# The last 96 rows of a down projection: chunks 0 and 1 in pieces of 32 rows, and the last token tile's feed-forward sum taken out of its bank whole

## The chip, the cores and the metric

The kernel runs on one core of one Trainium2 chip. The metric is the device time of one execution in microseconds (us). A kernel is executed several times and the median counts; one further execution is recorded by the hardware profiler, and all views below come from that one.

TensorE (PE) multiplies matrices into PSUM, which this kernel uses as eight banks of 128 x 512 fp32 values. ScalarE (ACT) and VectorE (DVE) read PSUM and work on SBUF. GpSimd (POOL) does a few small operations here and issues DMAs from its own queue, as SyncE (SP) and ACT do from theirs. Each engine and each queue works in order.

## The reference

For one sequence of 2048 tokens with 512 features the kernel adds a residual, a state-space layer and a gated feed-forward layer, the two layers both reading the layer-normed input:

```python
x = A_x                                   # 1 x 2048 x 512
xn = _layernorm(x, axis=-1)
# A: h[t] = Lam_bar * h[t-1] + B_bar xn[t] (complex, 512 states); y = 2 Re(C h) + xn * Dskip
# B: (silu(xn @ w_gate) * (xn @ w_up)) @ w_down        with F = 1376 hidden columns
return x + A(xn) + B(xn)
```

F = 1376 is 10 full tiles of 128 hidden columns and a remainder of 96. The change is about these 96 rows of `w_down`.

## The kernel before

**Tiles.** The 2048 tokens are 4 chunks (`NCH`) of 512 tokens (`CW`), each of 4 token tiles (`TPC`) of 128. Normed tokens lie transposed in `xnT`. Everything is written out by hand: an outer list of calls sets PE's order, and DVE's state-space work stands in a `backlog` that `pump` works off beside PE's matmuls and `need(tag)` forces to its end. The tile layer keeps this order and puts in the waits; the pool `psum` has 8 buffers, one per bank.

**Stages of a chunk.** `bproj_chunk(c)` projects the input to the states (32 matmuls, L371). `gateup_chunk(c)` makes gate and up of the feed-forward layer: first `gateup_last(c)` (L501, the remainder of 96 columns, packed into one bank with a part of up), then 10 tiles of 2 x 4 matmuls (L446). ACT takes each bank out (silu L460, copy L461), DVE multiplies pairs of them (L465). The product of the remainder stands in `gu_last` (96 rows x 512 tokens; `product_last`, L477). Then the down projection sums, for each token tile, 10 matmuls of 128 x 512 (L587 in `out_ffn` for chunks 0 and 1, L559 in `out_pair` for chunks 2 and 3) and the 96 remaining rows, and the 8 matmuls of the state-space output (L606, `out_ssm`) are added in the same bank.

**The remainder, two ways.** `out_last` (L594) multiplies it with one more matmul per token tile: `gu_last`, whose rows 96 to 127 are set to zero by DVE at the start (L170), against slice `FT - 1` of `wd_sb`. Chunk 1 does this in `out_ffn`. Chunk 0 does it late, in `out_end(0)`, after the first tile of chunk 2's gate and up, because the up part of its remainder is made only in `up_halves` (L490); until then its four sums stay in their banks. Chunks 2 and 3 do it in pieces (`out_rows`, L547): `move_rows` copies the product by 12 DMAs on POOL (L186) so that each of the four token tiles has its own group of 32 partitions, `load_rows` (L180, POOL) puts the 96 rows of `w_down` four times into the dead space of `BT`, and each of three steps then runs four matmuls of 32 rows, one for each token tile, in the four row groups of PE.

**The last token tile.** Tile 15 is summed in two column halves (`col_parts`): columns 256 to 511 first, closed by one `out_last` of 256 columns, then columns 0 to 255, for which the pieces are used. `part_end` (DVE, L575) takes the upper half out of the bank with the skip part added; the state-space matmuls of the last 256 columns run in two fresh banks of 128 columns (`out_blocks`), those of the first half go on in the old bank. L611 adds and casts, L614 stores.

**Leaving.** Chunks 0 to 2 leave through `out_leave`: an ACT copy (L619) into `res` (pool `opool`, 6 buffers) and a DMA on POOL that adds to `out` in DRAM (L620). `skip_store` (L530, POOL) adds the skip part the same way.

**PE's order around the change:** ... B-projection 2, `out_chunk(0)` = 40 x L587, `up_halves`, 32 x L606; gate and up of chunk 2 with `out_end(0)` in it; B-projection 3; `load_rows`; `out_chunk(1)` = 4 x (10 x L587 + 1 x L594), 32 x L606; gate and up of chunk 3; `out_pair(2)`.

Of the kernel before, what the change touches and what calls it, by code (L numbers as in the profile page):

```python
# [10 lines left out]
F32 = mybir.dt.float32  # L11
BF16 = mybir.dt.bfloat16
ALU = mybir.AluOpType
ACT = mybir.ActivationFunctionType
# [9 lines left out]
def kernel(  # L24
# [17 lines left out]
    nc = tc.nc  # L42
# [30 lines left out]
    def bank(shape=(128, CW), dtype=F32):  # L73
        return psum.tile(list(shape), dtype, name="ps")
# [18 lines left out]
        wu_g.append(const.tile([128, KD, cols], BF16, name=f"wu{gi}"))  # L93
    w_last = const.tile([128, KD, 128], BF16, name="w_last")
    wu_last = const.tile([128, KD, LB], BF16, name="wu_last")
    wd_sb = const.tile([128, FT, D], BF16, name="wd_sb")
    BT = const.tile([128, 2, KD, Pst], BF16, name="BT")
    CT = const.tile([128, 2, NQ, D], BF16, name="CT")
    dsk_bc = const.tile([128, D], BF16, name="dsk_bc")
# [48 lines left out]
    def load_late():  # L148
        nc.sync.dma_start(out=wu_last[:], in_=wu_v[:, :, FL:FL + LB])
        nc.sync.dma_start(out=xall[:, 2 * TPC:NT, :], in_=x_v[:, 2 * TPC:NT, :])  # L150
        nc.sync.dma_start(out=wd_sb[:, 0:nfull, :], in_=B_w_down[0:nfull * 128, :].rearrange("(k p) d -> p k d", p=128))
        if nfull < FT:
            nc.sync.dma_start(out=wd_sb[0:F - FL, nfull, :], in_=B_w_down[FL:F, :])

    nfull = F // 128


    ones = nc.const_aps.tensor(1.0, (128, CW), BF16)
# [6 lines left out]

    gu_last = [const.tile([128, CW], BF16, name=f"gu_last{i}") for i in range(3)]
    for t in (*(g[LB + LA:128, :] for g in gu_last), wd_sb[LB + LA:128, FT - 1, :]):
        nc.vector.memset(t, 0.0)  # L170


    RT = 32
    part_end = const.tile([128, D // 2], F32, name="part_end")
    gu_rows = [const.tile([128, 3, 128], BF16, name=f"gu_rows{i}") for i in range(2)]
    wd_rows = BT[:, 0, 0:3, :]

    def load_rows():
        for i in range(TPC):
            nc.gpsimd.dma_start(out=wd_rows[i * RT:(i + 1) * RT], in_=B_w_down[FL:F, :].rearrange("(p f) d -> f p d", f=RT))  # L180

    def move_rows(c):

        for i in range(TPC):
            for p in range(3):
                nc.gpsimd.dma_start(out=gu_rows[c % 2][i * RT:(i + 1) * RT, p, :],  # L186
                                    in_=gu_last[c % 3][p * RT:(p + 1) * RT, i * 128:(i + 1) * 128])

    stats = const.tile([128, NT, 6], F32, name="stats")
    stats_1 = const.tile([128, 2, 6], F32, name="stats_1")  # L190
# [278 lines left out]
    def ul(c):  # L469
        if c not in up_last:  # L470
            up_last[c] = up_p.tile([128, CW], BF16, name="ul", bufs=4)
        return up_last[c]

    def product_last(c):
        g, u = gu_last[c % 3][0:LB + LA, :], ul(c)[0:LB + LA, :]
        def mul():
            V.tensor_tensor(out=g, in0=g, in1=u, op=ALU.mult)  # L477
            if c > 1:
                move_rows(c)
        products.append(mul)  # L480

    def up_halves():
# [15 lines left out]
    def gateup_last(c):  # L498
        ps = bank()
        for k in range(KD):  # L500
            nc.tensor.matmul(ps[:], lhsT=w_last[:, k, :], rhs=xnT[:, k, c * CW:(c + 1) * CW],  # L501
                             start=(k == 0), stop=(k == KD - 1))
        u = ul(c)
        nc.scalar.activation(out=gu_last[c % 3][0:LB + LA, :], in_=ps[0:LB + LA], func=ACT.Silu)
        nc.scalar.copy(out=u[LB:LB + LA, :], in_=ps[LB + LA:128])
        if c > 1:
            product_last(c)
# [27 lines left out]
    def out_blocks(n):  # L535

        return ((0, D // 2), (D // 2, D - 128), (D - 128, D)) if n == NT - 1 else ((0, D),)

    def col_parts(n):
        return ((D // 2, D), (0, D // 2)) if n == NT - 1 else ((0, D),)  # L540

    def out_rows(c, step):

        for i in range(TPC):
            n, rows = c * TPC + i, slice(i * RT, (i + 1) * RT)
            lo, hi = col_parts(n)[-1]
            nc.tensor.matmul(o_tiles[n][0][:, lo:hi], lhsT=gu_rows[c % 2][rows, step, :],  # L547
                             rhs=wd_rows[rows, step, lo:hi], start=False, stop=False)

    def out_pair(c):  # L550

        multiply(0)
        for n in range(c * TPC, (c + 2) * TPC):
            o = bank()
            o_tiles[n] = [o]
            k, i = divmod(n, TPC)
            for lo, hi in col_parts(n):
                for fi in range(FT - 1):
                    nc.tensor.matmul(o[:, lo:hi], lhsT=gu_tiles[k][:, fi, i * 128:(i + 1) * 128],  # L559
                                     rhs=wd_sb[:, fi, lo:hi], start=(fi == 0), stop=False)  # L560
                if lo > 0:
                    out_last(n, o[:, lo:hi], lo, hi, True)
            pump(FT * 0.2163)
        for step in range(3):
            for k in (c, c + 1):
                out_rows(k, step)
        need(f"ssm{c}")
        need("skip")
        for n in range(c * TPC, (c + 1) * TPC):
            out_ssm(n)  # L570
            pump(2 * NQ * 0.2163)
        need(f"ssm{c + 1}")
        n = NT - 1
        o = o_tiles[n][0]
        V.tensor_tensor(out=part_end[:], in0=o[:, D // 2:D], in1=xn_end[:, TPC - 1, D // 2:D], op=ALU.add)  # L575
        o_tiles[n] = [o, *(bank((128, hi - lo)) for lo, hi in out_blocks(n)[1:])]
        for n in range((c + 1) * TPC, (c + 2) * TPC):
            out_ssm(n)

    def out_ffn(n):  # L580
        c, i = divmod(n, TPC)
        o_tiles[n] = []
        for lo, hi in out_blocks(n):
            o = bank((128, hi - lo))
            o_tiles[n].append(o)
            for fi in range(FT - 1):
                nc.tensor.matmul(o[:], lhsT=gu_tiles[c][:, fi, i * 128:(i + 1) * 128], rhs=wd_sb[:, fi, lo:hi],  # L587
                                 start=(fi == 0), stop=False)
            if c > 0:
                out_last(n, o, lo, hi, False)  # L590

    def out_last(n, o, lo, hi, stop):
        c, i = divmod(n, TPC)
        nc.tensor.matmul(o[:], lhsT=gu_last[c % 3][:, i * 128:(i + 1) * 128], rhs=wd_sb[:, FT - 1, lo:hi],  # L594
                         start=False, stop=stop)

    def out_ssm(n):
        c, i = divmod(n, TPC)
        if c > 0:
            res = opool.tile([128, D], BF16, name="res")  # L600
        for o, (lo, hi) in zip(o_tiles[n], out_blocks(n)):
            fresh = n == NT - 1 and lo > 0
            o = o[:, 0:hi - lo]
            for part in range(2):
                for q in range(NQ):
                    nc.tensor.matmul(o, lhsT=w_tiles[c][:, part, q, i * 128:(i + 1) * 128],  # L606
                                     rhs=CF[:, part, q, lo:hi], start=(fresh and part == 0 and q == 0),
                                     stop=(c > 0 and part == 1 and q == NQ - 1))
            if c == NCH - 1:
                rest = part_end[:, lo - D // 2:hi - D // 2] if fresh else xn_end[:, i, lo:hi]  # L610
                V.tensor_tensor(out=res[:, lo:hi], in0=o, in1=rest, op=ALU.add)  # L611
                for a, b in ((0, D // 2), (D // 2, D)) if i == 0 else ((lo, hi),):
                    late = b == D and n in (NT - TPC, NT - 1)
                    (nc.sync if late else nc.scalar).dma_start(out=out_v[:, n, a:b], in_=res[:, a:b])  # L614
            elif c > 0:
                out_leave(n, o, res)

    def out_leave(n, o, res):
        nc.scalar.copy(out=res[:], in_=o[:])  # L619
        nc.gpsimd.dma_start(out=out_v[:, n, :], in_=res[:], accum_op=ALU.add)  # L620
# [31 lines left out]
    def multiply(keep):  # L652

        while len(products) > keep:
            products.pop(0)()
            owed[0] -= 0.65

    def need(tag):

        while any(item[3] == tag for item in backlog):  # L660
            step()
# [98 lines left out]
    def gateup_chunk(c):  # L760
        for fi in [FT - 1, *range(FT - 1)]:
            gateup_tile(c, fi)
            pump(GU)
            multiply(1)
            if c == 2 and fi == 0:
                out_end(0)

    def out_chunk(c):

        multiply(0)  # L770
        for n in range(c * TPC, (c + 1) * TPC):
            out_ffn(n)
            pump(FT * 0.2163)
        if c == 0:
            need("ln3")
            up_halves()
            multiply(0)
        need(f"ssm{c}")
        need("cf")
        for n in range(c * TPC, (c + 1) * TPC):  # L780
            out_ssm(n)
            pump(2 * NQ * 0.2163)

    def out_end(c):

        for n in range(c * TPC, (c + 1) * TPC):
            o = o_tiles[n][0]
            out_last(n, o, 0, D, True)
            out_leave(n, o, opool.tile([128, D], BF16, name="res"))

    def spread(ops, others, tag, tags):

# [90 lines left out]
```

## Time and profile before

| | before |
|---|---|
| median of 3 runs | 178.83 us (178.77 to 179.09) |
| the profiled execution | 179.21 us |
| its span, first to last instruction | 177.4 us |
| around the span (179.21 - 177.4) | 1.8 us |
| PE busy | 173.1 us, 98% |
| DVE busy | 154.6 us, 87% |
| ACT busy | 93.8 us, 53% |
| POOL busy | 39.6 us, 22% |
| granted TensorE clock | 1.000 |

How to read the views. The chain of waits is the work that ended last, followed back from the end; each row is a start in us from the start of the span, a length in us, and what ran ("x8": eight instructions merged). The timeline of an engine has start, length, engine, line, operation, output<-inputs and shape, and in brackets the idle time before it with the engine that ended it. PEld is PE's load of weights. Groups by line give busy time, mean ns of one, and idle time before them. The list of DMA issues ends with the median time from issue to landing. Matmuls are pipelined: one of 512 columns is recorded as 379 ns long, but they start about 216 ns apart, so time on PE is counted here from start to start.

### The profile page before, as it was taken

The numbers are of one execution on the slowest core, as the hardware profiler recorded it, in microseconds if no ns is written. First come the engines' busy times: TensorE is split into PE (matmuls) and PEld (weight loads), VectorE is DVE, ScalarE is ACT, GpSimd is POOL, SyncE is SP. The second block draws the span as 40 slices with busy tenths as digits, with TensorE's granted clock in tenths as the row PEclk, the third lists the DMA queues.
The fourth block names the chain that finished last, engine by engine and source line by source line (L and its number), as shares of the span: only waits on it lengthen the run. The fifth ranks groups of instructions, "written<-read, shape, count | busy, mean of one in ns | idle before, by whom it ended". The sixth has DMA issues, their size and how long they took to land.

```text
span 177.4 us, 2510 instructions
## 1 busy us (share of the span) xinstructions
PE 173.1 (98%) x922; PEld 83.1 (47%) x922; DVE 154.6 (87%) x238; ACT 93.8 (53%) x167; POOL 39.6 (22%) x61
## 2 busy tenths in 40 slices
PE   7899999999999999999999999999999999999993
PEld 2784444444444444444444444444444444464443
DVE  6879997999999996899999999999999999991033
ACT  3558898967299649924966662013866610001300
POOL 6050300000300050000709340005186330001410
PEclk9999999999999999999999999999999999999999
DMA  5999857994141015900450011005569600000652
GB/s 172 277 260 202 177 98 142 345 222 105 28 88 34 0 30 118 355 0 0 46 76 15 9 49 43 0 0 59 59 87 181 105 9 0 0 0 4 65 98 76
DMA packets 30092, 16.13 MB, mean 91 GB/s; under 512 B 19296, under 2 KB 29888, under 8 KB 30048
## 3 DMA queue, kind: packets, MB, share of 16 engines
q1 hardware_dynamic: 24800, 11.54, 28.9%
q0 software_dynamic: 4416, 3.87, 15.7%
q10 hardware_dynamic: 864, 0.56, 1.0%
q8 instruction: 7, 0.11, 0.3%
q14 instruction: 5, 0.04, 0.1%
HBM read 8.42 MB, written 5.24 MB: 77 GB/s over the span
## 4 chain that ended last, share of the span: by engine, by line
PE 94%; DMA 3%; SPq 2%; issue 0%; DVE 0%
PE ps L446 36%; PE ps L606 16%; PE ps L371 16%; PE ps L559 10%; PE ps L587 10%; DMA wu<-in_B_w_up_dram 3%; PE ps L501 2%; PE ps L695 2%; PE ps L490 1%; PE ps L594 1%; PE ps L547 1%; SPq L112 1%; SPq L126 0%; SPq L127 0%; SPq L121 0%
## 5 line engine op out<-in xcount | busy, mean ns | idle before, releaser
L446 PE MATMUL ps<-xnT,wg 128*128 128x512 bf16 x148 | 38.0, 379 | 0.0
L446 PE MATMUL ps<-xnT,wu 128*128 128x512 bf16 x148 | 38.0, 379 | 0.0
L413 DVE TENSOR_TENSOR_SCAN g<-r_t,car,u 128x512 bf16<-128x512 f32 x24 | 28.7, 1262 | 0.0
L460 ACT ACTIVATE guT<-ps 128x512 bf16<-128x512 f32 x40 | 24.4, 611 | 7.3 <-PE ps L446 5.2
L371 PE MATMUL ps<-xnT,BT 128*128 128x512 bf16 x128 | 28.3, 379 | 0.0
L606 PE MATMUL ps<-CF,wt 128*128 128x512 bf16 (+2 forms) x144 | 28.2, 355 | 0.0
L461 ACT CAST u<-ps 128x512 bf16<-128x512 f32 x40 | 23.9, 599 | 5.4 <-PE ps L446 5.3
L619 ACT CAST res<-ps 128x512 bf16<-128x512 f32 x12 | 6.8, 594 | 37.5 <-PE ps L606 37.5
L620 POOL DMA_DIRECT2D out_dram<-res x12 | 10.5, 1044 | 59.3 <-ACT res L619 59.3
L446 PEld LDWEIGHTS <-wu 128*128 128x128 bf16 x148 | 14.5, 98 | 17.5
L446 PEld LDWEIGHTS <-wg 128*128 128x128 bf16 x148 | 14.4, 98 | 17.2
L373 ACT CAST u<-ps 128x512 bf16<-128x512 f32 x32 | 18.4, 590 | 5.1 <-PE ps L371 4.9
L606 PEld LDWEIGHTS <-wt 128*128 128x128 bf16 x144 | 13.3, 98 | 14.8 <-issue 0.4
L371 PEld LDWEIGHTS <-BT 128*128 128x128 bf16 x128 | 12.5, 98 | 15.1
L587 PE MATMUL ps<-wd_sb,guT 128*128 128x512 bf16 x80 | 18.1, 379 | 0.0
L559 PE MATMUL ps<-wd_sb,guT 128*128 128x512 bf16 (+1 forms) x90 | 17.6, 355 | 0.0
L211 POOL TENSOR_TENSOR rstd<-ve,neg_half 128x4 f32<-128x4 f32 x3 | 5.2, 1728 | 47.5 <-DVE ve L210 47.5
L186 POOL DMA_DIRECT2D gu_rows<-gu_last x24 | 11.9, 505 | 9.2 <-DVE gu_last L477 6.6
L465 DVE TENSOR_TENSOR guT<-guT,u 128x1024 bf16<-128x1024 bf16 x20 | 13.5, 681 | 0.0
L559 PEld LDWEIGHTS <-guT 128*128 128x128 bf16 x90 | 8.8, 98 | 8.7
L587 PEld LDWEIGHTS <-guT 128*128 128x128 bf16 x80 | 7.8, 98 | 9.4
L611 DVE TENSOR_TENSOR res<-ps,xn_end 128x512 bf16<-128x512 f32 (+1 forms) x4 | 2.5, 626 | 10.6 <-PE ps L606 10.6
(116 smaller groups left out, 196.6 us busy)
## 6 DMA issues: line engine op xcount, KB each, us to landing
out_dram<-in_A_x_dram SPq DMA_DIRECT2D x1, 1536.0 KB, 7.0
out_dram<-res POOLq DMA_DIRECT2D x12, 128.0 KB, 3.2
out_dram<-xall POOLq DMA_DIRECT2D x3, 512.0 KB, 8.2
wd_sb<-in_B_w_down_dram SPq DMA_DIRECT2D x1, 1280.0 KB, 10.2
xall<-in_A_x_dram SPq DMA_DIRECT2D x1, 1024.0 KB, 7.0
wg<-in_B_w_gate_dram SPq DMA_DIRECT2D x1, 512.0 KB, 6.0
wu<-in_B_w_up_dram SPq DMA_DIRECT2D x1, 512.0 KB, 6.9
xall<-in_A_x_dram SPq DMA_DIRECT2D x2, 256.0 KB, 7.1
```

The source lines that it names most:

```text
L186: nc.gpsimd.dma_start(out=gu_rows[c % 2][i * RT:(i + 1) * RT, p, :], in_=gu_last[c % 3][p * RT:(p + 1) * RT, i * 128:(i + 1) * 128])
L371: nc.tensor.matmul(ps[:], lhsT=BT[:, part, k, q * 128:(q + 1) * 128], rhs=xnT[:, k, c * CW:(c + 1) * CW], start=(k == 0), stop=(k == KD - 1))
L373: nc.scalar.copy(out=u_tiles[c][:, part, q, :], in_=ps[:])
L413: V.tensor_tensor_scan(out=g()[:, part, q, :], data0=r_t[:, q:q + 1].to_broadcast([128, CW]), data1=u_tiles[c][:, part, q, :], initial=ini ...
L446: nc.tensor.matmul(ps[:fs, lo:hi], lhsT=wslice(groups, fi, k), rhs=xnT[:, k, c * CW + lo:c * CW + hi], start=(k == 0), stop=(k == KD - 1))
L460: nc.scalar.activation(out=guT[:fs, fi, :], in_=psg[:fs], func=ACT.Silu)
L461: nc.scalar.copy(out=u_pair[c][:fs, fi % 2, :], in_=psu[:fs])
L465: products.append(lambda: V.tensor_tensor(out=g, in0=g, in1=u, op=ALU.mult))
L559: nc.tensor.matmul(o[:, lo:hi], lhsT=gu_tiles[k][:, fi, i * 128:(i + 1) * 128], rhs=wd_sb[:, fi, lo:hi], start=(fi == 0), stop=False)
L587: nc.tensor.matmul(o[:], lhsT=gu_tiles[c][:, fi, i * 128:(i + 1) * 128], rhs=wd_sb[:, fi, lo:hi], start=(fi == 0), stop=False)
L606: nc.tensor.matmul(o, lhsT=w_tiles[c][:, part, q, i * 128:(i + 1) * 128], rhs=CF[:, part, q, lo:hi], start=(fresh and part == 0 and q == 0 ...
L620: nc.gpsimd.dma_start(out=out_v[:, n, :], in_=res[:], accum_op=ALU.add)
```

## The change

The remainder of chunks 0 and 1 is no longer multiplied by `out_last`, which is gone with `out_end`, `col_parts`, the zeroed rows and slice `FT - 1` of `wd_sb`. `move_rows` now runs for all four chunks, each with its own `gu_rows` buffer; the products of chunks 0 to 2 are written to `ul` and not back to `gu_last`, of which there are two and not three. The four sums of chunk 0 stay in their banks until `out_chunk(1)`, where after the 40 matmuls of chunk 1 the pieces of chunks 0 and 1 run together (24 matmuls), chunk 0 leaves, and the state-space matmuls of chunk 1 follow. Tile 15 is summed over all 512 columns, with pieces of all 512; `part_end` takes out the whole bank, and all three column blocks of its state-space output start in fresh banks. The load of `wd_sb` is two DMAs of five slices.

```diff
-    wd_sb = const.tile([128, FT, D], BF16, name="wd_sb")
+    wd_sb = const.tile([128, FT - 1, D], BF16, name="wd_sb")
...
-        nc.sync.dma_start(out=wd_sb[:, 0:nfull, :], in_=B_w_down[0:nfull * 128, :].rearrange("(k p) d -> p k d", p=128))
-        if nfull < FT:
-            nc.sync.dma_start(out=wd_sb[0:F - FL, nfull, :], in_=B_w_down[FL:F, :])
+        wd_v = B_w_down[0:FL, :].rearrange("(k p) d -> p k d", p=128)
+        for a, b in ((0, FT // 2), (FT // 2, FT - 1)):
+            nc.sync.dma_start(out=wd_sb[:, a:b, :], in_=wd_v[:, a:b, :])
...
-    gu_last = [const.tile([128, CW], BF16, name=f"gu_last{i}") for i in range(3)]
-    for t in (*(g[LB + LA:128, :] for g in gu_last), wd_sb[LB + LA:128, FT - 1, :]):
-        nc.vector.memset(t, 0.0)
+    gu_last = [const.tile([128, CW], BF16, name=f"gu_last{i}") for i in range(2)]
...
-    part_end = const.tile([128, D // 2], F32, name="part_end")
-    gu_rows = [const.tile([128, 3, 128], BF16, name=f"gu_rows{i}") for i in range(2)]
+    part_end = const.tile([128, D], F32, name="part_end")
+    gu_rows = [const.tile([128, 3, 128], BF16, name=f"gu_rows{i}") for i in range(NCH)]
...
     def product_last(c):
-        g, u = gu_last[c % 3][0:LB + LA, :], ul(c)[0:LB + LA, :]
+        g, u = gu_last[c % 2][0:LB + LA, :], ul(c)[0:LB + LA, :]
         def mul():
-            V.tensor_tensor(out=g, in0=g, in1=u, op=ALU.mult)
-            if c > 1:
-                move_rows(c)
+            to = g if c == NCH - 1 else u
+            V.tensor_tensor(out=to, in0=g, in1=u, op=ALU.mult)
+            move_rows(c, to)
...
-            lo, hi = col_parts(n)[-1]
-            nc.tensor.matmul(o_tiles[n][0][:, lo:hi], lhsT=gu_rows[c % 2][rows, step, :],
-                             rhs=wd_rows[rows, step, lo:hi], start=False, stop=False)
+            nc.tensor.matmul(o_tiles[n][0][:], lhsT=gu_rows[c][rows, step, :], rhs=wd_rows[rows, step, :],
+                             start=False, stop=(step == 2 and (c == 0 or n == NT - 1)))
...
-            for lo, hi in col_parts(n):
-                for fi in range(FT - 1):
-                    nc.tensor.matmul(o[:, lo:hi], lhsT=gu_tiles[k][:, fi, i * 128:(i + 1) * 128],
-                                     rhs=wd_sb[:, fi, lo:hi], start=(fi == 0), stop=False)
-                if lo > 0:
-                    out_last(n, o[:, lo:hi], lo, hi, True)
+            for fi in range(FT - 1):
+                nc.tensor.matmul(o[:], lhsT=gu_tiles[k][:, fi, i * 128:(i + 1) * 128], rhs=wd_sb[:, fi, :],
+                                 start=(fi == 0), stop=False)
...
-        V.tensor_tensor(out=part_end[:], in0=o[:, D // 2:D], in1=xn_end[:, TPC - 1, D // 2:D], op=ALU.add)
-        o_tiles[n] = [o, *(bank((128, hi - lo)) for lo, hi in out_blocks(n)[1:])]
+        V.tensor_tensor(out=part_end[:], in0=o[:], in1=xn_end[:, TPC - 1, :], op=ALU.add)
+        o_tiles[n] = [bank((128, hi - lo)) for lo, hi in out_blocks(n)]
...
-            if c > 0:
-                out_last(n, o, lo, hi, False)
...
-            fresh = n == NT - 1 and lo > 0
+            fresh = n == NT - 1
...
-            if c == 2 and fi == 0:
-                out_end(0)
...
+        if c == 1:
+            for step in range(3):
+                for k in range(2):
+                    out_rows(k, step)
+            for n in range(TPC):
+                out_leave(n, o_tiles[n][0], opool.tile([128, D], BF16, name="res"))
```

More of the change, by code (lines that the diff above doesn't have):

```diff
@@ L150, in load_late @@
         nc.sync.dma_start(out=xall[:, 2 * TPC:NT, :], in_=x_v[:, 2 * TPC:NT, :])
-        nc.sync.dma_start(out=wd_sb[:, 0:nfull, :], in_=B_w_down[0:nfull * 128, :].rearrange("(k p) d -> p k d", p=128))
-        if nfull < FT:
-            nc.sync.dma_start(out=wd_sb[0:F - FL, nfull, :], in_=B_w_down[FL:F, :])
-    nfull = F // 128
+        wd_v = B_w_down[0:FL, :].rearrange("(k p) d -> p k d", p=128)
+        for a, b in ((0, FT // 2), (FT // 2, FT - 1)):
+            nc.sync.dma_start(out=wd_sb[:, a:b, :], in_=wd_v[:, a:b, :])
     ones = nc.const_aps.tensor(1.0, (128, CW), BF16)
@@ L180, in load_rows, with move_rows @@
             nc.gpsimd.dma_start(out=wd_rows[i * RT:(i + 1) * RT], in_=B_w_down[FL:F, :].rearrange("(p f) d -> f p d", f=RT))
-    def move_rows(c):
+    def move_rows(c, product):
         for i in range(TPC):
             for p in range(3):
-                nc.gpsimd.dma_start(out=gu_rows[c % 2][i * RT:(i + 1) * RT, p, :],
-                                    in_=gu_last[c % 3][p * RT:(p + 1) * RT, i * 128:(i + 1) * 128])
+                nc.gpsimd.dma_start(out=gu_rows[c][i * RT:(i + 1) * RT, p, :],
+                                    in_=product[p * RT:(p + 1) * RT, i * 128:(i + 1) * 128])
     stats = const.tile([128, NT, 6], F32, name="stats")
@@ L503, in gateup_last @@
         u = ul(c)
-        nc.scalar.activation(out=gu_last[c % 3][0:LB + LA, :], in_=ps[0:LB + LA], func=ACT.Silu)
+        nc.scalar.activation(out=gu_last[c % 2][0:LB + LA, :], in_=ps[0:LB + LA], func=ACT.Silu)
         nc.scalar.copy(out=u[LB:LB + LA, :], in_=ps[LB + LA:128])
@@ L537, in out_blocks @@
         return ((0, D // 2), (D // 2, D - 128), (D - 128, D)) if n == NT - 1 else ((0, D),)
-    def col_parts(n):
-        return ((D // 2, D), (0, D // 2)) if n == NT - 1 else ((0, D),)
     def out_rows(c, step):
@@ L588, in out_ffn @@
                                  start=(fi == 0), stop=False)
-            if c > 0:
-                out_last(n, o, lo, hi, False)
[L592 to L595, printed above, removed]
     def out_ssm(n):
@@ L609, in out_ssm @@
             if c == NCH - 1:
-                rest = part_end[:, lo - D // 2:hi - D // 2] if fresh else xn_end[:, i, lo:hi]
+                rest = part_end[:, lo:hi] if fresh else xn_end[:, i, lo:hi]
                 V.tensor_tensor(out=res[:, lo:hi], in0=o, in1=rest, op=ALU.add)
@@ L782, in out_chunk @@
             pump(2 * NQ * 0.2163)
[L784 to L789, printed above, removed]
     def spread(ops, others, tag, tags):
```

## The prediction

> **What bounds the kernel now.** The page comes first: is one engine the bound over the whole span?
>
> ```profile
> span 177.4 us, 2510 instructions
> PE 173.1 (98%) x922; PEld 83.1 (47%) x922; DVE 154.6 (87%) x238; ACT 93.8 (53%) x167; POOL 39.6 (22%) x61
> ```
>
> PE is. Whether DVE, at 87%, ends some wait of PE is answered by the chain of waits in order of time (start, length, what), here from the late stages:
>
> ```profile
> 64.01 8.63 PE ps L587 x40
> ...
> 82.37 1.73 PE ps L446 x8
> 84.09 0.86 PE ps L594 x4
> 84.96 15.54 PE ps L446 x72
> 100.50 6.91 PE ps L371 x32
> 107.40 2.16 PE ps L587 x10
> 109.56 0.22 PE ps L594
> ...
> 116.69 0.21 PE ps L594
> 116.90 6.91 PE ps L606 x32
> 123.81 0.86 PE ps L501 x4
> 124.67 17.27 PE ps L446 x80
> 141.94 16.20 PE ps L559 x80
> 158.14 0.11 PE ps L594
> 158.25 1.09 PE ps L559 x10
> 159.34 1.40 PE ps L547 x18
> 160.74 13.97 PE ps L606 x80
> ...
> 174.74 0.29 DVE res L611
> ```
>
> Each row begins where the one above ends, also where rows are left out, and all of it is PE until the last addition. So in this stretch a matmul taken away is time taken away, as long as PE finds its operands and banks ready 0.2 to 0.9 us sooner. The pace is 17.27 / 80 = 0.216 us for a matmul of 512 columns.
>
> **The change part by part.** *Removed from PE.* The four L594 at 84.09 stand in the chain with 0.86 us; the four of chunk 1, between 109.56 and 116.90, are 4 x 0.216 = 0.86; the one of 256 columns at 158.14 is 0.11. Tile 15's 20 half matmuls become 10 whole ones: the first half of them is 16.20 - 70 x 0.216 = 1.09, the second half 1.09 by its own row, so 2.18 against 2.16, 0.02 less. Sum removed: 0.86 + 0.86 + 0.11 + 0.02 = 1.85 us.
>
> *Added to PE.* 24 pieces of 32 rows. Before does the same thing once, for chunks 2 and 3, and the timeline around it (start, length, what) gives its price:
>
> ```profile
> 158.08 1.25 PE L559 MATMUL ps<-wd_sb,guT 128*128 128x256 bf16 x10
> 159.27 1.47 PE L547 MATMUL ps<-BT,gu_rows 32*128 32x512 bf16 x24
> 160.67 14.03 PE L606 MATMUL ps<-CF,wt 128*128 128x512 bf16 x80
> ```
>
> Six groups of four pieces, the four side by side, take 6 x 0.216 = 1.30 of the 1.40 us between the first piece and the first L606: the overlap is nearly complete. The rest is the change from whole-array to 32-row matmuls and back. Ahead of the pieces, ten L559 at 0.109 from 158.08 are through at 159.17, and the first piece starts at 159.27: 0.10. Behind, 1.40 - 1.30 = 0.10. So 24 pieces cost 1.50, counted from start to start. The chain says 1.40, because its row for L559 ends where the model puts that matmul's end, not where the next could start. I take 1.50, since it counts both switches; 1.40 is the lower end. As the upper end I take 1.60, another 0.10 for a switch behind 512-column matmuls, which no row shows.
>
> At this place the trace can be held against the Trainium skill, "TensorE: Matmul & The Clock Gate", section "Part 3: Packing small matmuls — row/col tiling": four row tiles of 32 rows at 512 columns were measured there 3.07 times as fast as one after the other. By that, an estimate from the page, the 24 pieces cost 24 x 0.216 / 3.07 = 1.69 and the change gains 0.16 us, 178.67. The rows here give 24 x 0.216 / 1.50 = 3.5 times, switches included, so the trace disagrees and I go by it.
>
> *The other pieces in the pair.* Tile 15's pieces grow from 256 to 512 columns. They run beside three others of 512 already, and the six groups hold the pace of 512: nothing.
>
> *Sum on PE:* -1.85 + 1.50 = **-0.35 us**, with -0.45 and -0.25 as ends.
>
> *What must not become late.* Four sums of chunk 0 hold four of the eight banks through chunk 2's gate and up and B-projection 3, until the pieces. ACT and DVE there:
>
> ```profile
> 82.40 0.59 ACT L504 ACTIVATE gu_last<-ps 96x512 bf16<-96x512 f32 x1 [6.05 <-PE ps L501]
> 84.61 2.06 ACT L619 CAST res<-ps 128x512 bf16<-128x512 f32 x4
> 98.81 0.59 ACT L461 CAST u<-ps 128x512 bf16<-128x512 f32 x1 [0.27 <-PE ps L446]
> 118.66 0.59 ACT L619 CAST res<-ps 128x512 bf16<-128x512 f32 x1 [10.64 <-PE ps L606]
> 82.06 0.75 DVE L477 TENSOR_TENSOR gu_last<-gu_last,ul 96x512 bf16<-96x512 bf16 x2
> 96.42 0.68 DVE L465 TENSOR_TENSOR guT<-guT,u 128x1024 bf16<-128x1024 bf16 x1
> 148.01 1.28 DVE L465 TENSOR_TENSOR guT<-guT,u 128x1024 bf16<-128x1024 bf16 x2
> 160.80 0.42 DVE L575 TENSOR_TENSOR part_end<-ps,xn_end 128x256 f32<-128x256 f32 x1 [0.73 <-PE ps L547]
> ```
>
> A bank is filled in 0.86 us and taken out in 0.59 right after, ACT waiting 0.27 for PE each time. With four banks the same one is wanted 3 x 0.86 = 2.6 after it was filled, and free after some 0.7: 1.9 us of slack. At the start it is less. With two `gu_last` buffers, L504 of chunk 2 must wait until L477 has read chunk 0's: 82.06 + 0.41 (half of 0.75, with its overlap), so about 82.5 and not 82.40. Its bank is freed after two ACT instructions, at 83.7, and wanted again at 82.37 + 3 x 0.86 = 84.95: 1.2 us of slack, and ACT has lost the four copies at 84.61. Queued behind L504 on ACT are the copies of tile 0, which find PE only just done. The up buffers go round in four: the copy for tile 8 of chunk 2 (98.81, now 97.95) needs the product that ends at 97.10; 0.85 of slack, and then the banks' 1.9. Chunk 3's products end at 149.29, and tile 12 wants its last one at 152.0 (141.7 + 8.63 for four token tiles + 1.7). All free, by these margins.
>
> POOL gets 24 more copies ahead of the load of the rows:
>
> ```profile
> 85.51 3.56 POOL L620 DMA_DIRECT2D out_dram<-res  x4 [20.81 <-ACT res L619]
> 93.39 5.94 POOL L186 DMA_DIRECT2D gu_rows<-gu_last  x12 [4.32 <-DVE gu_last L477]
> 104.03 2.18 POOL L180 DMA_DIRECT2D BT<-in_B_w_down_dram  x4 [4.70 <-PE ps L371]
> gu_rows<-gu_last POOLq DMA_DIRECT2D x24, 8.0 KB, 1.6
> BT<-in_B_w_down_dram POOLq DMA_DIRECT2D x4, 96.0 KB, 2.3
> out_dram<-res POOLq DMA_DIRECT2D x12, 128.0 KB, 3.2
> ```
>
> An issue takes 5.94 / 12 = 0.495. From 82.8, 24 of them run to 94.7, chunk 2's twelve to 100.6, and L180 still waits for PE at 104.03 - 0.86 = 103.2; it ends at 105.3 and lands by 107.7. The pieces start at 107.40 - 0.86 + 4 x 2.16 = 115.2. Slack 7.5 us. The four issues of chunk 0's output move from 85.51 to about 117, behind the pieces: copies 2.06 on ACT, issues 3.56 on POOL, the first landing 3.2 after issue, near 120.4. There are six `res` buffers, so tile 6's copy needs tile 0's DMA: it is due near 121.9 (118.66 + 2 x 1.73 - 0.2). 1.5 of slack, and ACT has nothing else until 124.
>
> *At nothing, and why:* `part_end` over 512 columns takes about 0.7 instead of 0.42 on DVE, at 160.8, where DVE's next work waits for tile 12 at 169; without that cover it would cost 0.3. Three fresh banks instead of two are those of tiles 8 to 10, empty by 167, and wanted at 173. The zeroing leaves DVE at the start, and the load of `wd_sb` changes shape:
>
> ```profile
> 1.22 0.82 DVE L170 MEMSET gu_last<- 32x256 uint32 x3
> 2.91 0.69 DVE L202 BATCH_NORM_STATS2 stats<-xall 128x6 f32<-128x512 bf16 x1 [0.59 <-DMA xall<-in_A_x_dram]
> 28.49 0.58 SPq L151 DMA_DIRECT2D wd_sb<-in_B_w_down_dram  x1
> ```
>
> DVE waits for the first tokens until 2.91 with the zeroing in front of it, and will wait longer without. `wd_sb` is issued at 28.5 and first read at 64.01, by the chain; two DMAs instead of two, 96 KB less.
>
> Against its own execution: 179.21 - 0.35 = 178.86. That execution lies 0.38 above the median of the runs, so against the median: 178.83 - 0.35 = **178.48 us**. A measurement of this kernel can tell about 0.2%, 0.36 us, from no change; the forecast lies on that line.
>
> **The rivals.**
>
> *A: the pieces overlap less in `out_chunk(1)`.* If each of the six groups paid a switch of 0.10, as the first does, they would cost 1.30 + 7 x 0.10 = 2.00: +0.15, 178.98. For it: chunk 0 and chunk 1 alternate in the same row groups. Against it: chunks 2 and 3 alternate just so, and their six groups hold the pace.
>
> *B, on the other side: PE runs out of banks at the start of chunk 2.* The place is the fifth group after the state-space output of chunk 0, which needs the bank that L504 empties. It decides from 1.2 us of lateness of L477. For it: DVE has no idle time in this stretch to catch up, and L477 ends only just as L504 could begin. Against it: nothing put ahead of L477 is new. If L477 came 2.4 us later, two of DVE's long products, PE would stand 1.2 us: +0.85, 179.7.
>
> *C: POOL is late with the rows.* If the 36 copies took 3.56 / 4 = 0.89 each, as output DMAs do, they would end at 114.8 and the rows land 4.5 later, at 119.3; PE waits 4.1 us: 182.6. It decides from (115.2 - 4.5 - 82.8) / 36 = 0.775 an issue. Against it: 0.495 in the row, beside a busy DVE.
>
> **How the numbers follow.** The forecast has 0.74: its terms are rows of the same operations, and every cover has a margin. Its ends are 178.38 and 178.58; with 0.15 for the run-to-run spread (178.77 to 179.09 in three), its own range is 178.2 to 178.75. It falls about 0.50 faster and 0.24 same, since 1.40 for the pieces is as well borne out by the chain as 1.60 is by nothing. A has 0.10 (same), B 0.11 and C 0.05 (slower). So faster 0.50, same 0.34, slower 0.16. The range runs from 178.1 to 179.2: the forecast, A, and a mild form of B.
>
> **What would show it.** Right: L594 gone; 24 L547 near 115.2 with about 1.50 from the last L587 to the first L606; `out_pair` starting near 141.7; no PE row broken between 84 and 107. Wrong: PE idle behind ACT in chunk 2 (B), L547 waiting for a DMA (C), the groups of L547 wider than 0.22 (A), or a later wait in `out_pair` that takes the 0.2 us back.

## The result, and the profile after

The changed kernel takes **178.53 us** (median of 21 runs, 178.36 to 178.98); the kernel before, run beside it 21 times, 178.83 us. The ratio is 0.9983, with a 95% interval of 0.9977 to 0.9989: 0.30 us faster, between 0.20 and 0.41. The forecast was 178.48 us and 0.35 us. The profiled execution took 178.79 us, with a span of 177.0.

First the page of the changed kernel, two of its lines:

```profile
span 177.0 us, 2543 instructions
PE 173.4 (98%) x927; PEld 82.3 (46%) x927; DVE 154.0 (87%) x234; ACT 94.2 (53%) x167; POOL 51.3 (29%) x85
```

PE bounds it as before. POOL has 24 instructions more and 11.7 us more to do. The chain of waits in order of time (start, length, what) shows what came of each stage; the lines of the code moved up, so L496, L441, L366, L575, L538, L587 and L549 are now the remainder's gate and up, gate and up, B-projection, down projection of chunks 0 and 1, pieces, state-space output, and down projection of chunks 2 and 3:

```profile
81.39 0.86 PE ps L496 x4
82.25 17.27 PE ps L441 x80
99.52 6.91 PE ps L366 x32
106.43 8.63 PE ps L575 x40
115.06 1.41 PE ps L538 x24
116.47 7.01 PE ps L587 x32
123.48 0.86 PE ps L496 x4
124.34 17.27 PE ps L441 x80
141.61 17.27 PE ps L549 x80
158.88 1.41 PE ps L538 x24
160.28 13.97 PE ps L587 x80
174.26 0.02 issue
174.28 0.29 DVE res L592
```

Chunk 2's gate and up is one row of 80 matmuls, where before the four L594 stood in it. From the row that begins at 82.25 (82.37 before) to the last addition it is 92.03 us, against 92.37: 0.34 less. The other 0.12 between the two profiles was there already at 82; it is looked at in the fourth experiment. The timeline of PE around the new pieces gives their price:

```profile
114.25 0.81 PE L575 MATMUL ps<-wd_sb,guT 128*128 128x512 bf16 x3
114.99 1.47 PE L538 MATMUL ps<-BT,gu_rows 32*128 32x512 bf16 x24
116.40 0.82 PE L587 MATMUL ps<-CF,wt 128*128 128x512 bf16 x3
```

The three L575 started 0.216 apart from 114.25, so the array was free again at 114.90; the pieces start at 114.99 and the next whole matmul at 116.40. That is 1.50 us, the forecast's number. ACT and DVE where four banks were held:

```profile
82.47 0.59 ACT L499 ACTIVATE gu_last<-ps 96x512 bf16<-96x512 f32 x1 [6.22 <-DVE ul L473]
97.83 0.59 ACT L456 CAST u<-ps 128x512 bf16<-128x512 f32 x1 [0.27 <-PE ps L441]
116.28 2.64 ACT L600 CAST res<-ps 128x512 bf16<-128x512 f32 x5 [9.23 <-PE ps L538]
81.96 0.75 DVE L473 TENSOR_TENSOR ul<-gu_last,ul 96x512 bf16<-96x512 bf16 x2
96.34 0.68 DVE L460 TENSOR_TENSOR guT<-guT,u 128x1024 bf16<-128x1024 bf16 x1
160.33 0.69 DVE L563 TENSOR_TENSOR part_end<-ps,xn_end 128x512 f32<-128x512 f32 x1 [0.37 <-PE ps L538]
```

The wait that two `gu_last` buffers bring is in the first row: what ended ACT's idle time is now DVE and no longer PE, at 82.47. Its bank was still free in time. From 85.7 us on ACT again waits 0.27 us for PE ahead of each bank, so ACT is ahead of PE through the rest of chunk 2's gate and up and of B-projection 3. The product at 96.34 ends 0.8 us before the copy at 97.83 wants its buffer. POOL:

```profile
82.67 17.59 POOL L181 DMA_DIRECT2D gu_rows<-ul  x36 [18.09 <-DVE ul L473]
103.06 0.56 POOL L175 DMA_DIRECT2D BT<-in_B_w_down_dram  x1 [2.79 <-PE ps L366]
103.91 1.65 POOL L175 DMA_DIRECT2D BT<-in_B_w_down_dram  x3 [0.29 <-issue]
117.17 6.40 POOL L601 DMA_DIRECT2D out_dram<-res  x7 [11.61 <-ACT res L600]
```

The 36 copies take 0.489 us each and are over at 100.3, and the load of the rows still waits for PE. Its last DMA landed at 107.34, 7.65 us before the first piece. Of chunk 0's output the first DMA landed at 120.37, and the copy of tile 6, which needs that `res` buffer, began at 121.83: the 1.5 us of the prediction.

### The profile page after: what moved, and what is told of

Read it like the earlier page. It is cut to its first block, busy times and chain, and to the rows that moved or that the text cites. A ratio compares the mean times of both kernels' runs of the same rounds, so it can differ in the third digit from the quotient of the medians.

```text
span 177.0 us, 2543 instructions
## 1 busy us (share of the span) xinstructions
PE 173.4 (98%) x927; PEld 82.3 (46%) x927; DVE 154.0 (87%) x234; ACT 94.2 (53%) x167; POOL 51.3 (29%) x85
## 4 chain that ended last, share of the span: by engine, by line
PE 96%; DMA 1%; DVE 1%; issue 0%
PE ps L441 36%; PE ps L587 16%; PE ps L366 16%; PE ps L575 10%; PE ps L549 10%; PE ps L676 3%; PE ps L496 2%; PE ps L538 2%; DMA xall<-in_A_x_dram 1%; PE ps L485 1%; PE ps L231 1%; DVE stats L197 0%; PE ps L653 0%; DVE xall L214 0%; DVE stats L684 0%; DVE res L592 0%
## 5 line engine op out<-in xcount | busy, mean ns | idle before, releaser
L441 PE MATMUL ps<-xnT,wu 128*128 128x512 bf16 x148 | 38.0, 379 | 0.0
L441 PE MATMUL ps<-xnT,wg 128*128 128x512 bf16 x148 | 38.0, 379 | 0.0
L366 PE MATMUL ps<-xnT,BT 128*128 128x512 bf16 x128 | 28.3, 379 | 0.0
L587 PE MATMUL ps<-CF,wt 128*128 128x512 bf16 (+2 forms) x144 | 28.2, 356 | 0.0
L181 POOL DMA_DIRECT2D gu_rows<-ul x36 | 17.6, 498 | 18.1 <-DVE ul L473 18.1
L441 PEld LDWEIGHTS <-wu 128*128 128x128 bf16 x148 | 14.5, 98 | 17.4
L441 PEld LDWEIGHTS <-wg 128*128 128x128 bf16 x148 | 14.4, 98 | 17.2
L587 PEld LDWEIGHTS <-wt 128*128 128x128 bf16 x144 | 13.3, 98 | 15.0 <-issue 0.8
L366 PEld LDWEIGHTS <-BT 128*128 128x128 bf16 x128 | 12.5, 98 | 15.1
L575 PE MATMUL ps<-wd_sb,guT 128*128 128x512 bf16 x80 | 17.6, 379 | 0.0
L549 PE MATMUL ps<-wd_sb,guT 128*128 128x512 bf16 x80 | 17.4, 379 | 0.0
L575 PEld LDWEIGHTS <-guT 128*128 128x128 bf16 x80 | 7.8, 98 | 9.4
L549 PEld LDWEIGHTS <-guT 128*128 128x128 bf16 x80 | 7.8, 98 | 9.5
L197 DVE BATCH_NORM_STATS2 stats<-xall 128x6 f32<-128x512 bf16 x14 | 9.5, 677 | 1.9 <-DMA xall<-in_A_x_dram 1.9
```

The lines of the kernel that those rows point to most:

```text
L181: nc.gpsimd.dma_start(out=gu_rows[c][i * RT:(i + 1) * RT, p, :], in_=product[p * RT:(p + 1) * RT, i * 128:(i + 1) * 128])
L366: nc.tensor.matmul(ps[:], lhsT=BT[:, part, k, q * 128:(q + 1) * 128], rhs=xnT[:, k, c * CW:(c + 1) * CW], start=(k == 0), stop=(k == KD - 1))
L441: nc.tensor.matmul(ps[:fs, lo:hi], lhsT=wslice(groups, fi, k), rhs=xnT[:, k, c * CW + lo:c * CW + hi], start=(k == 0), stop=(k == KD - 1))
L549: nc.tensor.matmul(o[:], lhsT=gu_tiles[k][:, fi, i * 128:(i + 1) * 128], rhs=wd_sb[:, fi, :], start=(fi == 0), stop=False)
```

## The experiments

Each kernel was timed against the kernel before in the same job. "Stretch" is from the start of the second group of remainder matmuls (38.81 us before, 38.70 in the changed kernel) to the start of PE's last matmul, both read from the timeline; it leaves out the start of the kernel, which differs between executions, and the end. "End" is from the start of PE's last matmul to the end of the span.

| kernel | ratio to before (95%) | stretch | end |
|---|---|---|---|
| before | | 135.672 | 2.96 |
| changed | 0.9983 (0.9977 to 0.9989) | 135.327 | 2.97 |
| banks held alone | 1.0001 (0.9992 to 1.0010) | 135.672 | 2.96 |
| last tile alone | 0.9991 (0.9981 to 1.0000) | 135.542 | 2.97 |
| chunks 0 and 1 alone | 0.9989 (0.9980 to 0.9998) | 135.456 | 2.97 |
| changed, old start | 0.9985 (0.9976 to 0.9993) | 135.325 | 3.04 |
| changed, two visits | 0.9991 (0.9982 to 1.0000) | 135.544 | 2.97 |
| changed, pieces by tile | 0.9980 (0.9971 to 0.9989) | 135.345 | 2.98 |
| changed, four idle ACT copies | 1.0079 (1.0060 to 1.0098) | 136.833 | 2.97 |
| changed, one idle ACT copy | 0.9984 (0.9975 to 0.9993) | 135.327 | 2.97 |
| changed, 24 more DMAs early | 1.0080 (1.0065 to 1.0096) | 136.335 | 3.66 |
| changed, 24 more DMAs later | 1.0030 (1.0018 to 1.0041) | 135.328 | 3.66 |

**1. The banks held, without the pieces.** On the kernel before:

```diff
-            if c == 2 and fi == 0:
-                out_end(0)
...
+        if c == 1:
+            out_end(0)
         need(f"ssm{c}")
         need("cf")
```

> The kernel before, with one thing moved: the four whole matmuls of chunk 0's remainder and its leaving come after the four token tiles of chunk 1 instead of inside chunk 2's gate and up, so that the four sums hold their banks as long as in the changed kernel. No pieces for chunks 0 and 1. Theory (time follows PE's count of matmuls and switches; four banks are enough): no change, 0.0 us with 0.1 either way against before, and no break in PE's row between 82 and 107 us. Rival (holding the banks costs, and the pieces gain more than counted): slower by 0.1 us or more, and PE waits for ACT in chunk 2. Second rival (the gain of the change comes from moving the four ACT copies out of chunk 2): faster by 0.2 us or more.

The stretch is the same to 0.001 us, and the ratio 1.0001. The four ACT copies went with it, from chunk 2 to 116. So neither does holding the banks cost anything, nor did it bring anything to take the copies out of chunk 2; both rivals fall.

**2. The last token tile alone.** On the kernel before, `col_parts` gives one part, `part_end` and the fresh banks cover all columns, and `opool` has 5 buffers:

```diff
-        return ((D // 2, D), (0, D // 2)) if n == NT - 1 else ((0, D),)
+        return ((0, D),)
...
-        V.tensor_tensor(out=part_end[:], in0=o[:, D // 2:D], in1=xn_end[:, TPC - 1, D // 2:D], op=ALU.add)
-        o_tiles[n] = [o, *(bank((128, hi - lo)) for lo, hi in out_blocks(n)[1:])]
+        V.tensor_tensor(out=part_end[:], in0=o[:], in1=xn_end[:, TPC - 1, :], op=ALU.add)
+        o_tiles[n] = [bank((128, hi - lo)) for lo, hi in out_blocks(n)]
...
-            fresh = n == NT - 1 and lo > 0
+            fresh = n == NT - 1
```

> The kernel before, with the last token tile alone changed: all 512 columns summed at once, its pieces over 512 columns, its bank taken out whole, three fresh banks; one output buffer fewer, so that it fits. Theory: one matmul of 256 columns (0.11 us) and the cost of halving (0.02) go, so -0.13 us against before, the first L606 of chunk 2 that much earlier. Rival (the larger take-out on DVE or the third fresh bank is on the path of the end): 0 or slower, with the last additions later after PE's last matmul than the 0.02 us of before.

The stretch is 0.13 us shorter and the end unchanged. The interval of the ratio reaches to 1.0000, so the time alone would not settle it; the trace does.

**3. Chunks 0 and 1 alone.** On the kernel before, `move_rows`, `product_last` and `gu_last` as in the change, the pieces in `out_chunk(1)`, no `out_end`, no L594 in `out_ffn`; the last token tile in halves with its `out_last`:

```diff
-            if c > 0:
-                out_last(n, o, lo, hi, False)
...
+        if c == 1:
+            for step in range(3):
+                for k in range(2):
+                    out_rows(k, step)
```

> The kernel before, with the pieces for chunks 0 and 1 alone; the last token tile in two column halves as before. Theory: eight matmuls go (-1.73 us) and 24 pieces with two switches come (+1.50), so -0.23 us against before. Together with the last tile's part this must give the whole. Rival (the gain sits in the last tile, and the pieces only pay for themselves): 0 to -0.1 us.

The stretch is 0.216 us shorter (0.23 forecast), and with the 0.130 of the last tile that makes 0.346, the whole of the change (135.672 - 135.327 = 0.345). The parts add up, so none hides another.

**4. The start as it was.** The changed kernel, with four zeroings on DVE and one load of `wd_sb`:

```diff
-        for a, b in ((0, FT // 2), (FT // 2, FT - 1)):
+        for a, b in ((0, FT - 1),):
...
+    for g in (*gu_last, *gu_last):
+        nc.vector.memset(g[LB + LA:128, :], 0.0)
```

> The changed kernel, with the start as it was: four zeroings of 32 rows on DVE, and one DMA for the ten slices of w_down. Theory: the start is bound by the DMA of the first tokens, so nothing: the same ratio to before as the changed kernel, about 0.998 (-0.3 us). Rival (the first gate-and-up matmul of 512 columns started 0.11 us earlier in the changed kernel's profile, and this is the zeroing that went): 0.1 us of the gain is given back, -0.2 us or less against before.

The ratio is that of the changed kernel, and the second remainder group begins at 38.32 us, earlier than the 38.70 of the changed kernel without any zeroing. Over all profiles of this study that moment lies between 38.26 and 39.01, with both ways of starting on both sides. The 0.12 us at the start of the two profiles shown is the spread of single executions and no part of the change.

**5. Two visits.** The changed kernel, the pieces in two places:

```diff
             out_ffn(n)
             pump(FT * 0.2163)
+            if n == TPC + 1:
+                for step in range(3):
+                    out_rows(0, step)
...
-                for k in range(2):
-                    out_rows(k, step)
+                out_rows(1, step)
```

> The changed kernel, with the twelve pieces of chunk 0 between the second and the third token tile of chunk 1, and the twelve of chunk 1 after the fourth: the same pieces, but PE changes to 32 rows and back twice. Theory (each change costs 0.10 us of PE): +0.20 us against the changed kernel, so -0.15 against before, and gaps of 0.10 us at all four places. Rival (the 0.10 ahead of and behind the pieces is the waits of the first piece and of the first state-space matmul, not the change of tiling): +0.10 us or less, since the chunk 1 matmuls in between wait for nothing.

The timeline of PE in this kernel, from 107.7 us on:

```profile
107.66 2.75 PE L575 MATMUL ps<-wd_sb,guT 128*128 128x512 bf16 x12
110.35 0.83 PE L538 MATMUL ps<-BT,gu_rows 32*128 32x512 bf16 x12
111.11 4.49 PE L575 MATMUL ps<-wd_sb,guT 128*128 128x512 bf16 x20
115.53 0.83 PE L538 MATMUL ps<-BT,gu_rows 32*128 32x512 bf16 x12
```

Three groups at 0.216 are 0.65 us; the first whole matmul after the first visit starts 0.76 after its first piece, and waits for nothing. The stretch is 0.22 longer than in the changed kernel for one visit more, 0.20 forecast. So 0.10 to 0.11 us is paid at each change of tiling, ahead of the pieces and behind them. PE's weight loads differ there. Among matmuls of one shape each load starts one matmul ahead (in the changed kernel at 114.466, for the matmul at 114.680). At a change, the first load of the new shape starts together with its own matmul, some 0.1 us after the array was free (at 114.988 and at 116.394). Whether the array is being emptied in this time, or only the load comes late, is not shown.

**6 and 7. The order of the pieces.** The changed kernel:

```diff
-    def out_rows(c, step):
+    def out_rows(c, step, tiles=range(TPC)):
...
-            for step in range(3):
-                for k in range(2):
-                    out_rows(k, step)
+            for k in range(2):
+                for i in range(TPC):
+                    for step in range(3):
+                        out_rows(k, step, (i,))
```

> The changed kernel, with the 24 pieces of chunks 0 and 1 in another order: the three of one token tile, which use the same row group, one after the other, then the next tile. Theory (pieces run side by side only with neighbours in another row group): two of three wait for the one before, 17 steps of 0.216 us instead of 6, +2.4 us against the changed kernel. Rival (PE's queue sorts it out): 0. Rival (nothing overlaps in this order): +3.9 us.

The theory failed, by all of its 2.4 us: the stretch is 135.345, 0.02 from the changed kernel's. The timeline of PE has the pieces in the same time, 1.44 us from 114.71 to where L587 could go on (its first record is missing there, one pace of 0.216 ahead of 116.37):

```profile
114.71 1.49 PE L538 MATMUL ps<-BT,gu_rows 32*128 32x512 bf16 x24
116.37 0.81 PE L587 MATMUL ps<-CF,wt 128*128 128x512 bf16 x3 [0.16 <-issue]
```

To see how, the same kernel with the pieces of token tile 3 cut to 256 columns, run once, for its trace alone:

```diff
+            hi = D // 2 if n == TPC - 1 else D
...
+            nc.tensor.matmul(o_tiles[n][0][:, 0:hi], lhsT=gu_rows[c][rows, step, :], rhs=wd_rows[rows, step, 0:hi],
```

> The kernel with the pieces by token tile, and the three pieces of token tile 3 cut to 256 columns, so that they can be told in the trace; its columns 256 to 511 lack the last 96 rows of the product. In the list of instructions they are the 10th to 12th of the 24. Theory (PE starts a piece of a free row group ahead of earlier ones whose row group is taken): one short piece in each of the first three groups of four, and the same 1.4 us from the first piece to the next whole matmul. Rival (PE starts in order, and pieces of one row group overlap as well): the short ones start 10th to 12th.

The matmuls of 32 rows, in order of their recorded starts (us; the length in ns tells the short ones), first nine:

```
115.303  385
115.313  384
115.323  385
115.333  277   short
115.453  268   short
115.530  374
115.539  374
115.550  374
115.562  267   short
```

In the program the short ones are the 10th to 12th. They start 4th, 5th and 9th, one behind the other, 0.11 to 0.12 us apart, in their own row group, while the other three groups run their long pieces. So PE starts a piece ahead of earlier ones whose row group is taken. From the first piece to where the next whole matmul could start it is 1.43 us (115.30 to 116.73, read as above), also as expected. The forecast's sum did not need the order `step`, then tile, that the code has; the overlap comes either way.

**8 and 9. The margin of the first bank.** The changed kernel, with idle copies on ACT behind the silu of chunk 2's remainder, first four of them:

```diff
         nc.scalar.activation(out=gu_last[c % 2][0:LB + LA, :], in_=ps[0:LB + LA], func=ACT.Silu)
+        if c == 2:
+            for _ in range(4):
+                nc.scalar.copy(out=part_end[:], in_=c16[:, 0, :])
```

> The changed kernel, with four idle ACT copies of 128 x 512 between the two ACT instructions that empty the first bank of chunk 2, about 2.5 us in all. Theory (with four banks held, that bank has 1.2 us of slack): PE stands once, about 1.3 us, ahead of the fifth group after the state-space output, and the whole is +1.3 us against the changed kernel. Rival (free banks are no limit there): 0. Rival (no slack at all): +2.5 us.

PE in this kernel, then ACT:

```profile
83.38 1.03 PE L441 MATMUL ps<-xnT,wg 128*128 128x512 bf16 x4
85.75 1.02 PE L441 MATMUL ps<-xnT,wu 128*128 128x512 bf16 x4 [1.34 <-ACT ul L503]
```

```profile
82.55 2.56 ACT L502 CAST part_end<-c 128x512 f32<-128x512 bf16 x4
85.12 0.58 ACT L503 CAST ul<-ps 32x512 bf16<-32x512 f32 x1
```

PE stands at the place and behind the instruction that rival B named. The group was due at 83.38 + 0.86 = 84.24 and starts at 85.75: 1.51 us late, and the stretch grew by the same 1.51. The same two instructions in the changed kernel:

```profile
83.07 0.58 ACT L500 CAST ul<-ps 32x512 bf16<-32x512 f32 x1
84.68 1.03 PE L441 MATMUL ps<-xnT,wu 128*128 128x512 bf16 x4
```

The bank is free at 83.65 and wanted at 84.68, 1.03 us later; in the run with the copies PE starts 0.05 after L503 ends (85.70 to 85.75), so the slack is 0.98. The delay gives the same. The four copies take 2.56 us of ACT, but L503 ends only 2.48 later than L500, counted from the start of chunk 2's remainder matmuls (4.91 us after 80.79 here, 2.43 after 81.23 in the changed kernel), since the first copy starts before the silu is over. 2.48 - 1.51 = 0.97. The bank has 1.0 us of slack, a little less than the 1.2 of the prediction and than the 1.05 in the next expectation, which took the 2.56 for the delay. With one copy (`range(1)`):

> The changed kernel, with one idle ACT copy (0.63 us) and not four between the two ACT instructions that empty the first bank of chunk 2. Four copies, 2.56 us of ACT, stood PE for 1.51 us, so that bank has 1.05 us of slack. Theory (the slack is a margin, and within it nothing is lost): 0, PE's row unbroken at the fifth group. Rival (each delay of that bank shows in part): +0.2 us or more.

Nothing: the stretch is the changed kernel's, and on PE the fifth group starts right behind the fourth:

```profile
83.41 1.03 PE L441 MATMUL ps<-xnT,wg 128*128 128x512 bf16 x4
84.27 1.03 PE L441 MATMUL ps<-xnT,wu 128*128 128x512 bf16 x4
```

The slack is a margin and not a slope.

**10 and 11. POOL.** The changed kernel, each copy of chunks 0 and 1 issued a second time into the buffer that chunk 3 will use:

```diff
+                if c < 2:
+                    nc.gpsimd.dma_start(out=gu_rows[3][i * RT:(i + 1) * RT, p, :],
+                                        in_=product[p * RT:(p + 1) * RT, i * 128:(i + 1) * 128])
```

> The changed kernel, with each copy of chunks 0 and 1 on POOL issued a second time into a buffer that is not yet in use: 60 issues ahead of the load of the rows instead of 36. Theory (0.49 us an issue, in order): the 60 end near 112.0, the rows land near 116.5, the pieces are due at 115.0: PE stands 1.5 us, +1.5 us against the changed kernel. Rival (the load of the rows is not held up, or the DMAs are the limit and not the issues): 0, or clearly more than 2 us.

Rows of POOL and of PE in this kernel:

```profile
111.67 2.20 POOL L175 DMA_DIRECT2D BT<-in_B_w_down_dram  x4
114.67 0.39 PE L541 MATMUL ps<-BT,gu_rows 32*128 32x512 bf16 x2
115.25 1.89 PE L541 MATMUL ps<-BT,gu_rows 32*128 32x512 bf16 x22 [0.20 <-DMA BT<-in_B_w_down_dram]
```

The load of the rows is held up as expected, to 111.67 (this execution is 0.32 us ahead of the changed kernel's). But the stretch grew by 1.01 us and not 1.5. The four DMAs of the load landed at 113.91, 114.55, 115.21 and 115.66. The first two pieces start when they are due, at 114.67; the third starts at 115.25 and the fourth at 115.70, each 0.04 after its row group's copy is there. The fifth, again in the first row group, starts only then as well, though what it reads had long landed: a piece that waits for its data holds back those behind it. So PE loses the time from 114.67 to the last landing, 0.99 us. The expectation had that landing too late: it added 2.2 us of issuing and 2.3 from issue to landing, but the 2.3 run from the start of an issue. From the start of the first issue to the last landing (111.67 to 115.66) it is 4.0 us and not 4.5. The time grew by 1.7 us (1.0080 against 0.9983), and the missing 0.69 stands at the end, where nothing was changed: 3.66 us against 2.97. The program's last line holds each engine's drain; from that line's list, in the kernels before, changed, and this one (min, median and longest in ns, first and last start in us):

```profile
L878 POOLq DRAIN  x3: 46/102/5042, 168.7 to 177.2; - x3
L878 SPq DRAIN  x3: 7/7/13, 176.6 to 176.9; - x3
```

```profile
L856 POOLq DRAIN  x3: 46/102/6748, 168.2 to 176.7; - x3
L856 SPq DRAIN  x3: 7/7/7, 176.2 to 176.5; - x3
```

```profile
L859 POOLq DRAIN  x3: 46/102/8705, 168.9 to 178.1; - x3
L859 SPq DRAIN  x3: 7/7/7, 176.8 to 177.8; - x3
```

The longest drain is POOL's first, begun with its last DMA. It grew by 1.7 us with the 24 DMAs of the change (47 on POOL before, 71 after) and by 1.96 with 24 more: 0.07 to 0.08 us for each DMA issued from POOL, though the last of the added ones had landed 60 us earlier. All profiles of this study agree: 4.99 to 5.14 us in the three kernels with 47, 6.75 in the eight with 71. The added DMAs are all copies of 8 KB, so whether their number counts, or their size, is not shown. SP's first drain stands behind the last store's landing. Before, POOL was through at 168.7 + 5.0 = 173.7, 2.9 us ahead of it; in the changed kernel at 174.9, 1.2 ahead; here at 177.6, 0.7 behind.

To part this from the late pieces, the 24 more copies were put behind the load of the rows, where POOL has nothing to do:

```diff
     def load_rows():
...
+        for c in range(2):
+            for i in range(TPC):
+                for p in range(3):
+                    nc.gpsimd.dma_start(out=gu_rows[3][i * RT:(i + 1) * RT, p, :],
+                                        in_=ul(c)[p * RT:(p + 1) * RT, i * 128:(i + 1) * 128])
```

> The changed kernel, with 24 more copies on POOL, but behind the load of the rows, where POOL has nothing to do until chunk 0 leaves: no piece waits. In the run with the copies doubled ahead of the load, PE lost 1.0 us and the time 1.6, and POOL's drain at the end of the kernel was 8.7 us long, after 6.7 in the changed kernel and 5.0 in the kernel before. Theory (the drain grows by some 0.08 us with each DMA that POOL has issued in the whole kernel, and ends the kernel once it outlasts the last stores, which leaves 1.2 us in the changed kernel): PE's row as in the changed kernel, a drain of 8.6 us that ends 0.7 us after the last store is seen, and +0.6 to +0.7 us against the changed kernel. Rival (the longer end came from PE being late, or the drain waits only for DMAs near the end): 0.

The drain of this kernel:

```profile
L861 POOLq DRAIN  x3: 46/102/8705, 168.3 to 177.5; - x3
L861 SPq DRAIN  x3: 7/7/13, 176.2 to 177.2; - x3
```

PE's stretch is that of the changed kernel; the drain is 8.7 us and ends at 176.97, 0.74 after SP's first begins (176.23); the end is 0.69 longer. The time is 0.84 us above the changed kernel's by the ratios (1.0030 and 0.9983), with intervals that hold 0.7. The rival falls.

## Why the prediction was right

*What bounds it.* Right. Work taken from PE after 82 us was time taken from the kernel, to 0.02 us in every kernel that only changed PE's list (experiments 1 to 3, 5 and 6).

*Removed, 1.85 us, and added, 1.50.* Right in sum and in parts. The pieces cost 1.50 from start to start in their new place too, as the first such row of the profile before had said, and 1.40 would have been wrong: two visits cost 0.22 more than one, and chunks 0 and 1 alone gained 0.216, which with 1.73 removed leaves 1.51 for the pieces. The ends of 1.40 and 1.60 were wider than needed. A switch behind matmuls of 512 columns costs the same as behind 256: 114.99 - 114.90 = 0.09.

*The rule of the Trainium skill* ("TensorE: Matmul & The Clock Gate", "Part 3: Packing small matmuls — row/col tiling", 3.07 times for four row tiles) would, by the estimate in the prediction, have had 24 pieces in 1.69 us. Measured are 24 x 0.216 / 1.50 = 3.5 times with the two switches, and 4 times between them.

*A, less overlap.* Did not happen, and experiment 6 shows that it would not have in another order either.

*B, the banks.* Did not happen; mechanism and place were right. The slack was 1.0 us and not 1.2: the prediction read the due time from the chain, whose row for gate and up begins 0.16 us after the recorded start of its first matmul (82.25 and 82.09), and left out the 0.05 that PE takes to go on. The wait of L499 for DVE was there, at 82.47.

*C, POOL.* Did not happen; the issue took 0.489 us and the load of the rows waited for PE. Two things in the price were off. The rows land 4.0 us after the first issue of their load begins and not 4.5 (experiment 10), so a late load costs half a microsecond less than was reckoned. And the prediction looked at POOL only up to the pieces: it did not see that each DMA there also lengthens POOL's drain at the end. That cover was never named. It hid 1.7 us, and 1.2 us of it is left. That the change did not pay for its DMAs there was luck, as far as the prediction goes.

*At nothing.* `part_end` took 0.69 us in DVE's idle time. The fresh banks and the load in halves left no trace. The zeroing brought nothing.

*The chances.* With 0.35 forecast against a line of 0.36, faster and same were not far apart. The greater chance, 0.50, stood on faster; the measured 0.30 us is clear of zero by its interval, but within 0.2%. PE's stretch says 0.345. That the median came to 0.05 us of 178.48 is in part luck: the median of the kernel before was 178.83 beside the changed kernel and 178.75 and 178.78 in the jobs of the experiments.

## What to carry to other kernels

Where one engine fills the chain from end to end, an edit's worth can be counted from start to start of its instructions, to a few hundredths of a microsecond; count the change of tiling on both sides of a packed block, and make one block of it. Then go through what each moved or added instruction holds up, queue by queue, and give each cover its margin in us: here 1.0 for a bank, 7.65 for the load of the rows, 1.2 for the drain. Do not stop at the last use: work that was put on a queue long before can still be paid for at the end of the kernel.

## What the runs showed of the hardware that was not expected

- POOL's drain at the end grows with the number of DMAs that it issued in the whole kernel: 5.0 us with 47, 6.7 with 71, 8.7 with 95, whether the added ones were issued between 82 and 107 us or between 105 and 117, and though all had landed some 50 us or more before. The added ones were all copies of 8 KB. It is free only while it is over before the last store has landed.
- PE takes matmuls of 32 rows out of the order of the program, so the sentence at the start that each engine works in order does not hold for them. With the three pieces of one row group next to each other in the list, four groups still ran side by side, and marked pieces listed 10th to 12th started 4th, 5th and 9th. Pieces behind one that waited for its data were not started ahead of it (experiment 10). How far ahead PE looks was not tried.
